# Residual matmuls moved between the gate and up matmuls of a decode kernel, and matmuls into an unread bank in PE's pauses there

## The chip, the cores and the metric

The kernel runs on one core of one Trainium2 chip. The metric is the time of one execution in microseconds of device time, as the median of several runs. A profile of one execution is there as well; all times with a decimal point that are called positions count from the first instruction of that execution.

## The reference

One decode step of a transformer block for 4 sequences (B = 4), one new token each, model width D = 576. The attention has 32 query heads and 16 key/value heads of 128, over the last 4096 of 16384 cached positions. Then follows a gated feed-forward layer of width F = 4608 with a ReLU gate.

```python
def _A_ref(x, k_cache, v_cache, wq, wo):
    W = min(4096, max(256, Sk // 4))
    q = (x @ wq).reshape(B, Sq, Hq, Dh).transpose(0, 2, 1, 3)
    k = jnp.repeat(k_cache[:, :, Sk - W:, :], rep, axis=1)
    v = jnp.repeat(v_cache[:, :, Sk - W:, :], rep, axis=1)
    scores = jnp.einsum("bhqd,bhkd->bhqk", q, k) * (Dh ** -0.5)
    p = _softmax(scores, axis=-1)
    o = jnp.einsum("bhqk,bhkd->bhqd", p, v)
    return o.transpose(0, 2, 1, 3).reshape(B, Sq, Hq * Dh) @ wo

def _B_ref(x, W_gate, W_up, W_down):
    gate = jnp.einsum("bsd,df->bsf", x, W_gate)
    up = jnp.einsum("bsd,df->bsf", x, W_up)
    gate = gate * (gate > 0)
    return jnp.einsum("bsf,fd->bsd", gate * up, W_down)

h = x + _A_ref(_layernorm(x), k_cache, v_cache, wq, wo)
h2 = h + _B_ref(_layernorm(h), W_gate, W_up, W_down)
```

Inputs and the output are bf16.

## The kernel before

The kernel is written engine by engine. Each of the five engines (SP, ACT, DVE, POOL, PE) has a function that issues its instructions in a fixed order, and a small class, Sched, turns the named dependencies into semaphore waits. Nothing is reordered by a planner: the order in prog_pe is the order on PE.

All large transfers are issued by prog_sync on SP's queue, one after the other, into one large SBUF buffer named pool: wq, then K and V of 32 pairs of heads, then wo in four parts, W_gate and W_up in four chunks of 128 rows of D each (named wg and wu, 0 to 3, alternating), then their last 64 rows (wg 4, wu 4), and at last W_down in nine pieces (wd 0 to 8). The first two pieces of W_down hold 9 chunks of 128 rows each, the next five 3 chunks each, and the last two hold 2 and 1. A transfer waits only for the buffer that it overwrites; for W_down that is the end of the output projection, called ATTN.

PE's work has these stages. First it computes q. Then it goes through the 32 pairs of heads: qk multiplies the transposed keys with the queries (matmuls of 512 columns into the four banks of the tile sc), and pv multiplies the probabilities with the values. The operand that holds the queries is the bf16 tile qz. After the last batch of heads comes the output projection, the statistics of the second layer norm, and then the feed-forward layer:

- For c from 0 to 3, 36 matmuls for the gate and 36 for the up projection, each with 128x128 weights and 4 moving columns, all into bank GUB. Each group of 36 waits for its own chunk of weights (`land((kind, c))`).
- Two groups of 18 matmuls with 8 moving columns, for the last 64 rows, gate and then up. The last one is named GU 4. ACT waits for it, applies the ReLU (A_GATE), and DVE multiplies (D_HHT) to make the tile hhT.
- Six fp32 matmuls that put the residual h, transposed back from the tile R_sb by the identity ident_f, into the banks DNB and DNB + 1. R_sb is there since the output projection (D_R).
- The down projection: 36 chunks of F, two matmuls each (one for each half of D, 288 columns, weights hhT of 128x4), which add to the residual in the two banks. The first waits for hhT and for wd 0; each further piece of W_down has its own wait.

At the end ACT and DVE copy one half each to bf16, and SP stores the result. Bank QR is the last of the four banks of sc; it holds the scores until the last softmax has read them, (EXP, 7, 1), and nothing reads it after that.

All matmuls other than the transposes are issued by the helper mm, so they share one line in the profile (L482), and are told apart by their tiles: pb<-hnT,pool and pb<-hn,pool are gate and up, pb<-ident_f,R_sb is the residual, pb<-pool,hhT the down projection.

Of the kernel before, what the change touches and what calls it, by code (L numbers as in the profile page):

```python
# [12 lines left out]
B = 4  # L13
D = 576
# [8 lines left out]
DC = 5  # L23
NDUO = B * KVH // 2
NB = 4
NBATCH = NDUO // NB
# [12 lines left out]
PVLAG = 5  # L39
JJ = 3  # L40
GD = 3
BIG = 1.5e38
NG = FC // JJ
HALF = F // 2
HD = D // 2
# [57 lines left out]
def bass_sequential_preLN__sliding_block_cached__glu_gated_reglu__decode_kernel(  # L103
# [12 lines left out]
    with ExitStack() as es:  # L116
        cnt = [0]

        def sb(name, shape, dt):
            return es.enter_context(nc.sbuf_tensor(name, shape, dt))  # L120
# [4 lines left out]
        ident_f = sb("ident_f", [128, 128], FP32)  # L125
# [17 lines left out]
        qz = sb("qz", [128, 2, NB, 4, 128], BF16)  # L143
# [18 lines left out]
        R_sb = sb("R_sb", [128, 2, DC, B], FP32)  # L162
# [9 lines left out]
        pb = [sc[:, i * 512:(i + 1) * 512] for i in range(4)]  # L172
        pb += [es.enter_context(nc.psum_tensor(f"pb{i}", [128, 512], FP32))[:, :] for i in range(4, 8)]
        PVB, OB, QB, QR, TPB = 4, 6, 6, 3, 7
        OSB, WOB, STB, GUB, DNB = 0, 1, 2, 7, 4
# [50 lines left out]
        for c in range(4):  # L226
            for k, (kind, W) in enumerate((("wg", B_W_gate), ("wu", B_W_up))):
                add((kind, c), f"{kind}{c}", GU0 + (2 * c + k) * ROW, F, None,
                    lambda e, o, c=c, W=W: e.dma_start(out=o, in_=W[c * 128:(c + 1) * 128, :]))
# [4 lines left out]
        wd_sb = pool[:, 0:FC * D].rearrange("p (g x) -> p g x", g=NG)  # L234
        WD = [(0, GD * JJ), (GD * JJ, 2 * GD * JJ)] + [(g * JJ, (g + 1) * JJ) for g in range(2 * GD, NG - 1)] + [(FC - JJ, FC - 1), (FC - 1, FC)]
        for k, (f0, f1) in enumerate(WD):
# [7 lines left out]
        def land(name):  # L244
            return ("L",) + (name if isinstance(name, tuple) else (name,))
# [99 lines left out]
        def prog_dve(S):  # L345
# [17 lines left out]
            for x in range(2):  # L363
# [3 lines left out]
                                              axis=AX.X, op=ALU.add), name="M0")  # L367
            S.op(v, lambda e: e.tensor_scalar(out=mask[:, 1, :], in0=mask[:, 0, :], scalar1=2 * BIG, scalar2=-BIG, op0=ALU.mult, op1=ALU.add),
                 deps=["M0"], name="M1")
            S.op(v, lambda e: e.tensor_scalar(out=mask[:, 2, :], in0=mask[:, 0, :], scalar1=-2 * BIG, scalar2=BIG, op0=ALU.mult, op1=ALU.add),  # L370
                 name="M2")
# [106 lines left out]
        def prog_pe(S):  # L478
            t = "tensor"

            def mm(o, l, r, start, stop, deps=(), name=None, skip=False):
                S.op(t, lambda e: e.matmul(o, lhsT=l, rhs=r, start=start, stop=stop, skip_group_check=skip),  # L482
                     deps=deps, name=name, signal=name is not None)

            for k, (src, base) in enumerate(((xn_bf, 0), (x_bf, 32))):
                for c in range(DC):
                    w = 128 if c < 4 else 64
# [3 lines left out]
                        deps=["A_XN", "IDB", land("x")] if k == 0 and c == 0 else [], name="TP1" if last else None, signal=last)  # L491
            mm(pb[STB][:, 0:B], dup[:, :], x4[:, :], True, True, deps=["D_XNT", "DUP"], name="XDUP")
            first = True
            for c in range(4):
                s = at[("wq", c)]
                for h in range(H):
                    mm(pb[QB][:, h * B:(h + 1) * B], pool[:, s + h * DH:s + (h + 1) * DH], xnT[:, c, :], first, False,
                       deps=[land(("wq", c))] + (["D_XNT"] if first else []) if h == 0 else [], skip=True)
                    first = False
            s = at[("wq", 4)]  # L500
            for h in range(H // 2):
                o = pb[QB][:, 0:H * B].rearrange("p (u x) -> p u x", u=2)[:, :, h * B:(h + 1) * B]
                mm(o, pool[:, s + h * DH:s + (h + 1) * DH], xn4[:, :, :], False, h == H // 2 - 1,
                   deps=[land(("wq", 4)), "XN41"] if h == 0 else [],
                   name="QMM" if h == H // 2 - 1 else None, skip=True)
            for ce in range(4):
                mm(pb[QR][:, ce * 128:(ce + 1) * 128], sel[:, ce, :, :].rearrange("p g k -> p (g k)"), qT_sb[:, :], True, True,
                   deps=["D_QT", "SEL3"] if ce == 0 else [], name="QREP" if ce == 3 else None)
# [55 lines left out]
            for e_ in range(4):  # L564
                for h4 in range(4):
                    mm(pb[OSB][32 * h4:32 * h4 + 32, e_ * 32:(e_ + 1) * 32], ident_b[:, e_:128:4],
                       oT_all[:, :, :].rearrange("p (q h) b -> p h q b", h=4)[:, h4, :, :], True, True,
                       deps=[("NORM", b) for b in range(B)] if e_ == 0 and h4 == 0 else [],
                       name="OSEL" if e_ == 3 and h4 == 3 else None)
            for g in range(NWO):  # L570
                wv = pool[:, at[("wo", g)]:at[("wo", g)] + ROW].rearrange("p (q e n) -> p q e n", q=2, e=4)
                deps = [land(("wo", g))] + (["D_OX"] if g == 0 else [])
                for n in range(DC):
                    w = 128 if n < 4 else 64
                    for q in range(2):
                        for e_ in range(4):
# [3 lines left out]
                            deps = []  # L580
            mm(pb[STB][:, 128:168], ones_f[:, :], R_sb[:, :, :, :], True, True, deps=["D_R"], name="STAT")
            mm(pb[STB][:, 256:256 + B], dup[:, :], hnT[0:64, 4, :], True, True, deps=["N2"], name="HDUP")
            first = True
            gub = pb[GUB][:, 0:2 * FC * B].rearrange("p (u x) -> p u x", u=2)

            def cols(ap, fc):
                g, j = divmod(fc, JJ)
                x0 = g * 128 * JJ + j
                return ap[:, x0:x0 + 127 * JJ + 1:JJ]

            for c in range(4):
                for u, kind in ((0, "wg"), (1, "wu")):
                    s = at[(kind, c)]
                    for f in range(FC):
                        mm(gub[:, u, f * B:(f + 1) * B], cols(pool[:, s:s + F], f), hnT[:, c, :], first, False,
                           deps=[land((kind, c))] + (["N2"] if first else []) if f == 0 else [], skip=True)
                        first = False
            for u, kind in ((0, "wg"), (1, "wu")):
                o = gub[:, u, :].rearrange("p (v x) -> p v x", v=2)
                for f in range(FC // 2):  # L600
                    last = u == 1 and f == FC // 2 - 1
                    mm(o[:, :, f * B:(f + 1) * B], cols(pool[:, at[(kind, 4)]:at[(kind, 4)] + HALF], f), hn4[:, :, :], False, last,
                       deps=[land((kind, 4)), "HN41"] if f == 0 else [], name=("GU", 4) if last else None, skip=True)
            first = True
            for u in range(2):
                for c in range(DC):
                    lo, hi = max(c * 128, u * HD), min(c * 128 + 128, D, (u + 1) * HD)
                    if lo < hi:
                        w = 128 if c < 4 else 64
                        mm(pb[DNB + u][0:B, lo - u * HD:hi - u * HD], R_sb[0:w, 0, c, :], ident_f[0:w, lo - c * 128:hi - c * 128],  # L610
                           c * 128 <= u * HD, False, deps=["D_R", "IDF"] if u == 0 and c == 0 else [], skip=True)
            for k, (f0, f1) in enumerate(WD):
                deps = [land(("wd", k))] + (["D_HHT"] if k == 0 else [])
                for f in range(f0, f1):
                    g, j = divmod(f, JJ)
                    for u in range(2):
                        last = f == FC - 1
                        mm(pb[DNB + u][0:B, 0:HD], hhT[:, f, :], wd_sb[:, g, j * D + u * HD:j * D + (u + 1) * HD], False, last,
                           deps=deps, name=f"DOWN{u}" if last else None, skip=True)
                        deps = []  # L620

        progs = [("gpsimd", prog_pool), ("sync", prog_sync), ("scalar", prog_act), ("vector", prog_dve), ("tensor", prog_pe)]
        S.begin(False)
        for _, p in progs:
# [33 lines left out]
```

## Time and profile before

| | |
|---|---|
| median of 3 runs | 384.68 us (384.5, 384.68, 385.1) |
| the profiled execution's own time | 385.3 us |
| its span, first to last instruction | 383.5 us |
| mean granted TensorE clock | 0.907 |
| busy: PE, DVE, ACT, POOL | 75%, 52%, 13%, 2% of the span |
| read from HBM | 159.58 MB, 416 GB/s over the span |
| down projection | 72 matmuls in 10.5 us, mean record 315 ns |
| gate and up, 4 columns | 288 matmuls, 8.8 us busy, 9.8 us idle before them |

The profiled execution's time has 1.8 us that lie outside its span. [...] The granted clock is the share of full speed at which TensorE ran; a table by stretches of time gives it for any stretch that one asks for. Records of matmuls overlap; the time that one costs in a row is the distance of their starts.

### The profile page before, as it was taken

To read this page: it belongs to the slowest core of one execution; us is meant where nothing else is said; L and a number is where in the kernel's file an instruction comes from. 1 tells how busy PE (TensorE), PEld (TensorE's weight loads), DVE (VectorE), ACT (ScalarE), POOL (GpSimd) and SP (SyncE) were. 2 spreads that over 40 slices of the span, in tenths; PEclk is the share of its full clock that TensorE was granted. 3 is DMA by queue.
4 is the path that set the end of the run, shared out by engine and by line. 5 is a ranking of instruction groups with operands and counts; after the bars stand their busy time and mean duration, and the time that the engine had idled before them with its cause. 6 is when DMAs were issued, how large, how long until landed. Compare 5 with 4: busy or idle time off the path is not lost.

```text
span 383.5 us, 4157 instructions
## 1 busy us (share of the span) xinstructions
PE 288.7 (75%) x1827; PEld 130.2 (34%) x1842; DVE 198.8 (52%) x181; ACT 51.5 (13%) x125; POOL 7.9 (2%) x20
## 2 busy tenths in 40 slices
PE   0059649976996699679958994899499788874387
PEld 0053213322432243224322431343134233374355
DVE  0259789269437854774486558645855450011000
ACT  4021040021102110311030004100400021100000
POOL 4000000000000000000000000000000000000000
PEclk9999958998999899989998999899989998955559
DMA  7999999999999999999999999999999999999994
GB/s 316 426 424 426 431 424 432 426 424 431 426 424 434 424 427 431 426 427 431 426 427 434 424 424 434 427 424 432 427 424 434 426 423 434 403 417 424 414 415 172
DMA packets 14306, 159.86 MB, mean 417 GB/s; under 512 B 1480, under 2 KB 1616, under 8 KB 4560
## 3 DMA queue, kind: packets, MB, share of 16 engines
q1 hardware_dynamic: 14280, 159.59, 98.6%
q8 instruction: 14, 0.23, 0.2%
q10 hardware_dynamic: 8, 0.00, 0.0%
q14 instruction: 4, 0.03, 0.0%
HBM read 159.58 MB, written 0.00 MB: 416 GB/s over the span
## 4 chain that ended last, share of the span: by engine, by line
PE 41%; DMA 23%; issue 15%; DVE 14%; ACT 5%; POOL 1%; SPq 0%; POOLq 0%
PE sc L482 23%; PE pb L482 18%; DMA pool<-in_A_k_cache_dram 9%; DMA pool<-in_B_W_down_dram 7%; DMA pool<-in_A_wo_dram 7%; ACT P L323 4%; DVE kT L394 4%; DVE probT L413 4%; DVE rmx L397 4%; POOL bcm L274 1%; DVE bias L409 0%; DVE rowsum L418 0%; DVE t L405 0%; DVE pmax L400 0%; DVE bmin L407 0%
## 5 line engine op out<-in xcount | busy, mean ns | idle before, releaser
L394 DVE STREAM_TRANSPOSE kT<-pool 128x2048 f32<-128x2048 f32 x64 | 144.5, 2291 | 54.6 <-DMA pool<-in_A_k_cache_dram 49.4
L482 PE MATMUL sc<-kT,qz 128*128 128x512 bf16 x497 | 131.9, 418 | 51.2 <-DVE kT L394 47.6
L482 PE MATMUL pb<-pool,prob 128*16 128x512 bf16 x512 | 116.4, 386 | 0.8 <-DMA pool<-in_A_v_cache_dram 0.8
L482 PEld LDWEIGHTS sc<-kT,qz 128*128 128x128 bf16 x512 | 49.0, 102 | 130.9 <-DVE kT L394 57.0
L482 PEld LDWEIGHTS pb<-pool,prob 128*16 128x16 bf16 x512 | 43.5, 91 | 71.0 <-issue 15.3
L323 ACT ACTIVATE P<-sc,bias 128x512 f32<-128x512 f32 x32 | 22.2, 714 | 176.5 <-DVE bias L409 176.5
L397 DVE TENSOR_REDUCE rmx<-sc 128x2 f32<-128x2048 f32 x8 | 18.3, 2292 | 34.0 <-PE sc L482 34.0
L413 DVE STREAM_TRANSPOSE probT<-P 128x2048 f32<-128x2048 f32 x8 | 18.5, 2311 | 7.8 <-ACT P L323 7.8
L482 PE MATMUL pb<-hnT,pool 128*128 128x4 bf16 x288 | 8.8, 167 | 9.8 <-DMA pool<-in_B_W_up_dram 5.0
L489 PE MATMUL pb<-ident_b,xn_bf 4*128 4x4 bf16 (+1 forms) x5 | 0.4, 175 | 20.3 <-ACT xn_bf L287 20.3
L308 ACT COPY cp<-pb 128x512 f32<-128x512 f32 x8 | 4.7, 584 | 67.5 <-PE pb L482 67.5
L482 PEld LDWEIGHTS pb<-hnT,pool 128*128 128x128 bf16 x288 | 8.2, 104 | 10.3 <-DMA pool<-in_B_W_up_dram 5.2
L422 DVE RECIPROCAL rs_sb<-pb 128x32 f32<-128x32 f32 x4 | 1.4, 338 | 19.8 <-PE pb L482 19.8
L482 PE MATMUL pb<-selT,cp 128*128 128x16 f32 x64 | 7.9, 255 | 4.3 <-ACT cp L308 4.3
L473 DVE TENSOR_TENSOR hhT<-pb,gate_sb 128x144 bf16<-128x144 f32 x1 | 0.3, 308 | 20.9 <-ACT gate_sb L339 20.9
L330 ACT CAST prob<-probT 128x1024 bf16<-128x1024 f32 x8 | 8.4, 1044 | 19.0 <-DVE rs L416 19.0
L482 PE MATMUL pb<-pool,hhT 128*4 128x288 bf16 x72 | 10.5, 315 | 0.4 <-DMA pool<-in_B_W_down_dram 0.4
L482 PEld LDWEIGHTS pb<-selT,cp 128*128 128x128 f32 x64 | 8.2, 191 | 6.3 <-ACT cp L308 5.3
L274 POOL PARTITION_ALL_REDUCE bcm<-pmax x8 | 3.1, 386 | 290.6 <-DVE pmax L400 290.6
L301 ACT COPY qz<-qrep 32x64 bf16<-32x64 bf16 x32 | 7.8, 245 | 7.3 <-DVE qrep L431 7.0
L482 PEld LDWEIGHTS pb<-pool,hhT 128*4 128x4 bf16 x72 | 6.6, 93 | 4.3 <-DMA pool<-in_B_W_down_dram 0.7
L489 PEld LDWEIGHTS pb<-ident_b,xn_bf 4*128 4x128 bf16 (+1 forms) x5 | 0.3, 108 | 20.3 <-ACT xn_bf L287 20.3
(94 smaller groups left out, 71.5 us busy)
## 6 DMA issues: line engine op xcount, KB each, us to landing
pool<-in_A_k_cache_dram SPq DMA_DIRECT2D x32, 2048.0 KB, 28.1
pool<-in_A_v_cache_dram SPq DMA_DIRECT2D x32, 2048.0 KB, 26.1
pool<-in_A_wo_dram SPq DMA_DIRECT2D x4, 1152.0 KB, 21.7
pool<-in_B_W_gate_dram SPq DMA_DIRECT2D x4, 1152.0 KB, 25.7
pool<-in_B_W_up_dram SPq DMA_DIRECT2D x4, 1152.0 KB, 24.5
pool<-in_A_wq_dram SPq DMA_DIRECT2D x4, 1024.0 KB, 7.9
pool<-in_B_W_down_dram SPq DMA_DIRECT2D x2, 1296.0 KB, 27.2
pool<-in_B_W_down_dram SPq DMA_DIRECT2D x5, 432.0 KB, 14.5
```

Of the source, the lines that this page charges most:

```text
L274: S.op(g, lambda e, n=n: e.partition_all_reduce(bcm[:, n % 2, :], pmax[:, n % 2, :], 128, bass_isa.ReduceOp.max), deps=deps, name=("PAR", n))
L301: S.op(a, lambda e, src=src, dst=dst: e.copy(out=dst, in_=src), deps=deps, name=("QZ", n) if g == 3 else None, signal=g == 3)
L308: S.op(a, lambda e: e.copy(out=cp[:, n % 2, :], in_=pb[PVB + n % 2]), deps=deps, name=("CP", n))
L323: S.op(a, lambda e, n=n, th=th, u=u: e.activation(out=P[:, th * 1024 + u:(th + 1) * 1024:2], in_=sc[:, th * 1024 + u:(th + 1) * 1024:2], f ...
L330: S.op(a, lambda e, n=n: e.copy(out=prob[:, n % 2, :, :, :], in_=probT[:, :, 0:NHB].rearrange("p t (r x) -> p r t x", x=4)), deps=deps, na ...
L394: S.op(v, lambda e: e.transpose(out=dst, in_=src), deps=deps, name=("TR", i))
L397: S.op(v, lambda e: e.tensor_reduce(out=rmx[:, n % 2, :], in_=sc[:, :].rearrange("p (x u) -> p u x", u=2), axis=AX.X, op=ALU.max), deps=[( ...
L413: S.op(v, lambda e: e.transpose(out=probT[:, :, :].rearrange("p t j -> p (t j)"), in_=P[:, :]), deps=[("EXP", n, 1)] + ([("CMP", n - 1)] i ...
L422: S.op(v, lambda e: e.reciprocal(out=rs_sb[:, b, :], in_=pb[OB][:, 64 + b * H:64 + (b + 1) * H]), deps=[("SUM", b)], name=("RS", b))
L473: S.op(v, lambda e: e.tensor_tensor(out=hhT[:, :, :], in0=pb[GUB][:, FC * B:2 * FC * B].rearrange("p (f b) -> p f b", b=B), in1=gate_sb[:, ...
L482: S.op(t, lambda e: e.matmul(o, lhsT=l, rhs=r, start=start, stop=stop, skip_group_check=skip), deps=deps, name=name, signal=name is not None)
L489: S.op(t, lambda e, c=c, w=w, src=src, base=base: e.transpose(out=tpv[0:w, base + c * 4:base + (c + 1) * 4], in_=src[0:B, c * 128:c * 128 ...
```

## The change

The residual's six matmuls become a function, residual(u), that is called for u = 0 just ahead of the gate matmuls of chunk 3 and for u = 1 just ahead of its up matmuls. A new function, warm(k), issues k bf16 matmuls of 128x128 weights and 512 columns, both operands taken from qz, into bank QR, which nothing reads any more. Its only dependency is the last softmax's reading of that bank. It is called with the numbers of the list WARM: the first after each of the two halves of the residual, the second ahead of the last gate group, the third ahead of the last up group, and the fourth ahead of the down projection. The list sums to seven; as its first number is used twice, eight such matmuls are issued. No other engine's program changes, and the order of everything else on PE stays.

```diff
+WARM = (1, 1, 2, 3)
...
+            def warm(k):
+                for _ in range(k):
+                    mm(pb[QR], qz[:, 0, 0, 0, :], qz[:, 1, 0, :, :].rearrange("p c m -> p (c m)"), True, True,
+                       deps=[("EXP", NBATCH - 1, 1)], skip=True)
+
+            def residual(u):
+                first = True
+                for c in range(DC):
+                    lo, hi = max(c * 128, u * HD), min(c * 128 + 128, D, (u + 1) * HD)
+                    if lo < hi:
+                        w = 128 if c < 4 else 64
+                        mm(pb[DNB + u][0:B, lo - u * HD:hi - u * HD], R_sb[0:w, 0, c, :], ident_f[0:w, lo - c * 128:hi - c * 128],
+                           c * 128 <= u * HD, False, deps=["D_R", "IDF"] if first else [], skip=True)
+                        first = False
+
             for c in range(4):
                 for u, kind in ((0, "wg"), (1, "wu")):
                     s = at[(kind, c)]
+                    if c == 3:
+                        residual(u)
+                        warm(WARM[0])
                     for f in range(FC):
                         mm(gub[:, u, f * B:(f + 1) * B], cols(pool[:, s:s + F], f), hnT[:, c, :], first, False,
                            deps=[land((kind, c))] + (["N2"] if first else []) if f == 0 else [], skip=True)
                         first = False
             for u, kind in ((0, "wg"), (1, "wu")):
                 o = gub[:, u, :].rearrange("p (v x) -> p v x", v=2)
+                warm(WARM[1 + u])
                 for f in range(FC // 2):
                     last = u == 1 and f == FC // 2 - 1
                     mm(o[:, :, f * B:(f + 1) * B], ...
-            first = True
-            for u in range(2):
-                for c in range(DC):
...
-                        mm(pb[DNB + u][0:B, lo - u * HD:hi - u * HD], R_sb[0:w, 0, c, :], ident_f[0:w, lo - c * 128:hi - c * 128],
-                           c * 128 <= u * HD, False, deps=["D_R", "IDF"] if u == 0 and c == 0 else [], skip=True)
+            warm(WARM[3])
             for k, (f0, f1) in enumerate(WD):
                 deps = [land(("wd", k))] + (["D_HHT"] if k == 0 else [])
```

## The prediction

> **What bounds the kernel now.** I read the page's strip of slices first. DMA is saturated in every slice but the first and the last, and PE's clock, at full speed or near it through the attention, falls to half for the end.
>
> ```profile
> PEclk9999958998999899989998999899989998955559
> DMA  7999999999999999999999999999999999999994
> ```
>
> Then the chain of waits, its last pieces (start, us, what):
>
> ```profile
> 343.77 26.88 DMA pool<-in_B_W_down_dram
> 370.64 0.04 issue
> 370.69 10.55 PE pb L482 x72
> 381.24 0.02 issue
> 381.26 0.45 DVE out_sb L475
> ```
>
> Until 370.64 the transfers set the time. From there the 72 matmuls of the down projection run without a pause. The last piece of W_down is issued at 367.93 and its row gives 12.2 us to landing, so it is there at 380.13; PE ends at 381.24. What can be gained or lost lies in this tail, and depends on PE's clock in it.
>
> Third, the table by stretches. The clock changes at 336.35 and 373.90, which are 37.55 us apart, eleven times 3.413; the changes during the attention fit the same grid. So I cut the trace into cells of 3.413 us (columns: stretch, length, PE busy, PEld, DVE, ACT, POOL, granted clock, DMA share, GB/s).
>
> ```profile
> 49.63:53.05 3.42, 1.93 (x5) 0.73 (x6) 2.71 (x2) 2.11 (x7) 0.00 (x0) 0.50 1.03 441
> 53.05:56.46 3.41, 1.67 (x4) 0.30 (x2) 3.38 (x4) 1.93 (x5) 0.00 (x0) 0.50 1.00 423
> ```
>
> ```profile
> 278.33:281.74 3.41, 2.81 (x7) 1.00 (x8) 1.83 (x2) 0.00 (x0) 0.00 (x0) 0.50 1.02 432
> 281.74:285.15 3.41, 3.41 (x16) 1.27 (x15) 3.22 (x2) 0.00 (x0) 0.00 (x0) 1.00 0.98 418
> ```
>
> ```profile
> 339.77:343.18 3.41, 3.34 (x96) 3.20 (x93) 0.00 (x0) 0.00 (x0) 0.00 (x0) 0.50 1.02 424
> ...
> 363.66:367.07 3.41, 1.77 (x54) 1.60 (x54) 0.00 (x0) 0.00 (x0) 0.00 (x0) 0.50 1.02 412
> 367.07:370.49 3.42, 2.75 (x30) 1.63 (x30) 0.31 (x1) 0.29 (x1) 0.00 (x0) 0.50 1.02 417
> 370.49:373.90 3.41, 3.21 (x14) 1.76 (x15) 0.00 (x0) 0.00 (x0) 0.00 (x0) 0.50 1.02 411
> 373.90:377.31 3.41, 3.41 (x30) 2.34 (x28) 0.00 (x0) 0.00 (x0) 0.00 (x0) 1.00 0.94 377
> ```
>
> What a cell did decides the clock of the next. The cell at 339.77 is busy for 3.34 us with matmuls 4 columns wide and stays at half: time in which columns stream counts, not busy time. A share of 1.93/3.41 = 0.57 did not raise the clock, 2.81/3.41 = 0.82 did. The threshold lies between. The cell at 367.07 narrows it: the residual matmuls stream 1.92 us (below), the 18 narrow ones 0.12, together 0.60, and the clock stays at half. So between 0.60 and 0.82; 0.70 is my middle.
>
> The rates, from the timeline:
>
> ```profile
> 368.10 2.17 PE L482 MATMUL pb<-ident_f,R_sb 128*4 128x128 f32 x12
> ...
> 370.88 1.89 PE L482 MATMUL pb<-pool,hhT 128*4 128x288 bf16 x7
> ...
> 375.18 1.39 PE L482 MATMUL pb<-pool,hhT 128*4 128x288 bf16 x10
> ```
>
> At half clock (1.89 - 0.447 of the last one)/6 = 0.2405 us from start to start, 0.835 ns a column; at full clock (1.39 - 0.286)/9 = 0.1227.
>
> **Check of the tail.** The clock rises 3.21 us after the first down matmul: 13.4 matmuls at half clock, 58.6 x 0.1227 = 7.19, and 0.16 until the last result: 370.69 + 3.21 + 7.19 + 0.16 = 381.25; measured 381.24. Each us more at half clock costs 1 - 0.1227/0.2405 = 0.49 us. The floor: the second piece is issued at 346.27 and lands after 27.5 (the longest of its rows), 373.8; its matmuls and all behind it, 54 x 0.1227 = 6.63, plus 0.16, give 380.6; the last piece at 380.13 and its two matmuls give the same. So up to about 1.9 us at half clock are free, and the most that any clock can save here is 381.24 - 380.6 = 0.65 us.
>
> **The change, part by part.** *Residual moved.* Six fp32 matmuls, recorded as 12 passes with 1152 columns at twice 0.835 ns: 1.92 us (row: 2.17 with the tail of the last). In two halves of 0.96 they now stand ahead of the gate and the up matmuls of chunk 3. Their inputs are ready since 344.2, and only PE's queue is concerned. They used to run from 368.10 to 370.27, while PE waited for 370.64: moving them out saves nothing on the path. *Added matmuls.* The list says 1, 1, 2, 3, and its first entry is issued twice: eight of 512 columns, 512 x 0.835 = 0.43 us each at half clock. Ahead of gate and up of chunk 3 the pauses are 1.66 us, and 0.96 + 0.43 = 1.39 fits. Ahead of chunk 4's gate the pause is 0.32: 0.11 late. Ahead of its up 0.77: two take 0.85, and the up matmuls end about 0.2 late, at 368.4. Relu (0.29) and product (0.31) follow, so hhT is there at 369.1, covered until 370.64; without that cover it would be 0.2 us. The last three end by 369.7, before anything waits for PE. So all the inserted work is free, at 0, and no transfer moves.
>
> *The clock.* In the profile's own cells the new content of 367.07 to 370.49 is: two fillers from 367.07 on 0.6, narrow 0.12, three fillers 1.28: 2.0 us, 0.58, no more than the 0.60 before. It would stay at half, the next cell (filled from 370.69) raises the clock at 373.90 as now, and the change is worth nothing. But this rests on where the grid lies. Call x the time from the first down matmul to the next cell edge (3.21 in the profile). [...] I take x as anything from 0 to 3.41; the timed runs, from 384.5 to 385.1, leave room for this.
>
> Before, the cell that ends at x holds the residual's 1.92 close ahead of the down matmuls: (2.04 + x)/3.41 up to x = 0.8, then above 0.8. At a threshold of 0.70 the clock rises at x for every x above 0.36, and half of these are within the free 1.9 us; the mean loss over the floor is about 0.2. After, the fillers give less, and 1.0 us of idle PE lies ahead of the down matmuls: the share is 0.52 at x = 0, about 0.64 from 0.9 to 2.3, then x/3.41. For x below about 1.7 the clock comes a cell later, 3.4 to 5.1 us after the first matmul, 0.75 to 1.6 over the floor (mean 1.15); between 1.7 and 2.3 the cell before holds 0.70 and may just raise it, at the floor; above 2.4 it is as before (about 0.5). Weighted: 0.52 x 1.15 + 0.30 x 0.5 = 0.75, or 0.55 more than before. A threshold of 0.63 gives 0.3 more, one of 0.77 gives 0.75. I take 0.45. On the median of 384.68 that is 385.1. (The profiled execution took 385.3 for a span of 383.5, 1.8 outside it; its floor would be 384.65, and 384.5 is the fastest timed run, so the median sits just above the floor.)
>
> [...]
>
> **The rivals.** *It works as filler:* the fillers raise the clock in nearly every execution before 372.5, and PE ends at the floor: 384.5, 0.2 under the median. For: with a threshold near 0.60 the plateau of 0.64 is enough. Against: the row with 0.60 that wasn't. Chance 0.24, of which 0.06 that the comparison's runs of before lie as high as the profiled one, so that it shows as over 0.2%. *Clearly slower:* the threshold is 0.75 or more, so that nothing short of the down matmuls raises the clock, and the moved residual takes away what did: for x from 0.7 to 2.7 the clock comes 4.1 to 6.1 us after the first matmul, 1.1 to 2.0 over the floor: about 385.9. It decides from a threshold of 0.74. Chance 0.28. *Nothing happens:* x is always near the profile's; 384.7. Chance 0.08. *My forecast,* a loss under 0.2%: 0.40.
>
> **The numbers.** 0.2%, 0.77 us, is about what a measurement of this kernel can tell from no change; the gain is bounded at 0.65 us, the loss at about 1.9. Faster 0.06; within 0.18 + 0.08 + 0.40 = 0.66; slower 0.28. The range goes from just under the floor, 384.4, to the third case's 386.0; my forecast's own range is 384.8 to 385.4.
>
> **What would show it.** In the profile after: the fillers inside the former pauses; the chain still ending with W_down and 72 matmuls from 370.7; hhT before 369.2; a cell with a share under 0.60 never followed by clock 1.00, one over 0.82 always; the matmuls' end at 381.25 - 0.49 x (3.21 - time at half clock), never under 380.6. Wrong would be: a first down matmul later than 370.8, a transfer that lands elsewhere, a clock that rises after cells that stream under 0.6, or a time under 384.2.

## The result and the profile after

The changed kernel takes 385.64 us (median of 14 runs, 384.59 to 386.39), the kernel before 384.69 (14 runs beside it, 384.31 to 385.36). The medians are 0.95 us apart; the ratio, which is that of the means, is 1.0021 with a 95% interval of 1.0013 to 1.0030: about 0.8 us slower. The forecast was 385.1 in a range of 384.4 to 386.0: the direction and the mechanism are the ones forecast, the size was put at half.

The profiled execution of the changed kernel took 385.91 us, with a span of 384.1. Its chain of waits ends as before (start, us, what):

```profile
343.73 26.70 DMA pool<-in_B_W_down_dram
370.42 0.04 issue
370.46 11.40 PE pb L483 x72
381.86 0.02 issue
381.88 0.45 DVE out_sb L476
```

No transfer and no wait is late: the first piece of W_down is there at 370.42 (370.64 before), and the first down matmul starts with it. But the 72 matmuls take 11.40 us in place of 10.55. The table by cells of 3.413 us, cut at this execution's own clock changes (337.86 and 375.40, 37.54 us or eleven cells apart), says why (columns as in the tables above; the granted clock is the third figure from the end):

```profile
361.75:365.16 3.41, 3.41 (x69) 2.24 (x70) 0.00 (x0) 0.00 (x0) 0.00 (x0) 0.50 1.00 404
365.16:368.58 3.42, 3.16 (x56) 1.80 (x55) 0.28 (x1) 0.29 (x1) 0.00 (x0) 0.50 1.03 418
368.58:371.99 3.41, 2.19 (x9) 0.85 (x8) 0.03 (x1) 0.00 (x0) 0.00 (x0) 0.50 1.02 410
371.99:375.40 3.41, 3.41 (x16) 1.78 (x14) 0.00 (x0) 0.00 (x0) 0.00 (x0) 0.50 1.03 417
375.40:378.82 3.42, 3.42 (x30) 2.37 (x28) 0.00 (x0) 0.00 (x0) 0.00 (x0) 1.00 0.71 282
```

The edge after the first down matmul is at 371.99, so x is 1.53 here. The cell that ends there holds the end of the fillers (to about 369.0), a pause, and 1.5 us of down matmuls; it streams about 2.0 us, a share of 0.58, and the clock is 0.50 for a whole further cell. PE runs 4.94 us at half clock in place of 3.21.

### The profile page after: what moved, and what is told of

It reads as the page before. It is cut to its first block, busy times and chain, and to the rows that moved or that the text cites. A ratio compares the mean times of both kernels' runs of the same rounds, so it can differ in the third digit from the quotient of the medians.

```text
span 384.1 us, 4171 instructions
## 1 busy us (share of the span) xinstructions
PE 297.7 (78%) x1833; PEld 133.1 (35%) x1850; DVE 199.0 (52%) x181; ACT 51.5 (13%) x125; POOL 7.9 (2%) x20
## 4 chain that ended last, share of the span: by engine, by line
PE 46%; DVE 18%; issue 15%; DMA 14%; ACT 6%; POOL 1%; POOLq 0%
PE sc L483 25%; PE pb L483 22%; DMA pool<-in_B_W_down_dram 7%; DMA pool<-in_A_wo_dram 7%; DVE kT L395 6%; ACT P L324 5%; DVE probT L414 4%; DVE rmx L398 4%; POOL bcm L275 1%; DVE bias L410 0%; DVE rowsum L419 0%; DVE pmax L401 0%; DVE t L406 0%; DVE bmin L408 0%; ACT qz L302 0%
## 5 line engine op out<-in xcount | busy, mean ns | idle before, releaser
L483 PE MATMUL sc<-kT,qz 128*128 128x512 bf16 x497 | 134.8, 426 | 47.9 <-DVE kT L395 44.4
L483 PE MATMUL pb<-pool,prob 128*16 128x512 bf16 x512 | 118.0, 391 | 0.0
L483 PE MATMUL pb<-pool,hhT 128*4 128x288 bf16 x72 | 11.4, 331 | 1.2 <-DMA pool<-in_B_W_down_dram 1.2
L483 PE MATMUL pb<-selT,cp 128*128 128x16 f32 x64 | 8.7, 269 | 4.3 <-ACT cp L309 4.3
L483 PEld LDWEIGHTS pb<-selT,cp 128*128 128x128 f32 x64 | 9.0, 208 | 6.3 <-ACT cp L309 5.3
```

## The experiments

Two theories. The share theory is the prediction's: the clock is granted cell by cell, by the share of the cell before in which columns stream, and what the change does is to empty the cell ahead of the down projection by moving the residual out of it. (A filler is one of the matmuls that `warm` issues; x is, as in the prediction, the time from the first down matmul to the next cell edge.) The rival, called the filler theory, is that the fillers cost time themselves, by holding PE's queue or by disturbing the transfers.

**e1: the residual moved, no fillers.**

```diff
-WARM = (1, 1, 2, 3)
+WARM = (0, 0, 0, 0)
```

> The change's residual in its new places, all eight fillers left out. Share theory (a 3.413 us cell decides the next cell's clock by the share in which columns stream, threshold between 0.62 and 0.82, and the residual's move emptied the cells ahead of the down projection): only the down matmuls themselves can raise the clock, so it is as slow as the change or a little slower, 0.9 to 1.1 us over the floor of 384.4 on average against 0.2 to 0.4 before: 385.5, and single runs spread over about 1.7 us. Filler theory (the eight fillers cost time themselves, by holding PE's queue or disturbing the transfers): without them it is as before, 384.7.

Measured: 385.45 (384.57 to 386.35), ratio to before 1.0016, interval 1.0002 to 1.0030. Most or all of the loss is there without any filler, which is against the filler theory. The interval only just leaves 1 out; e4 below decides. In its profile:

```profile
369.21:372.63 3.42, 2.24 (x10) 1.24 (x11) 0.00 (x0) 0.00 (x0) 0.00 (x0) 0.50 1.03 412
372.63:376.04 3.41, 3.41 (x16) 1.81 (x15) 0.00 (x0) 0.00 (x0) 0.00 (x0) 0.50 1.02 412
376.04:379.45 3.41, 3.41 (x30) 2.36 (x28) 0.00 (x0) 0.00 (x0) 0.00 (x0) 1.00 0.55 214
```

The down matmuls start at 370.39 and fill 2.24/3.41 = 0.66 of the cell, and the next cell is still at 0.50. Behind that one, which is full, the clock is 1.00.

**e2, e3, e4, e7, e8: the stretch ahead of the down projection made dense again.** e2 puts the residual back behind the last up matmuls and keeps the five fillers ahead of it:

```diff
-                        residual(u)
                         warm(WARM[0])
...
+            residual(0)
+            residual(1)
             warm(WARM[3])
-WARM = (1, 1, 2, 3)
+WARM = (1, 1, 2, 0)
```

> The residual back in its old place behind the last up matmuls; five fillers (1, 1, 1, 2) in the pauses ahead of it, none behind it. Share theory: the residual's 1.92 us stream just ahead of the down matmuls again, and the fillers before it add to the same cells: mean 0.1 to 0.25 over the floor, 384.6 (as before or 0.1 faster). Filler theory: five of the eight fillers keep five eighths of the loss, 385.2.

e3 is e2 with one filler behind the residual:

```diff
-WARM = (1, 1, 2, 0)
+WARM = (1, 1, 2, 1)
```

> As e2 with one filler more behind the residual, so that PE streams without a pause from the last up matmuls to the first down matmul. Share theory: every place of the grid has a cell with a share over 0.82 that ends before or soon after the first down matmul: every run at the floor, 384.4, with a spread of 0.3 us or less, 0.3 us faster than before. Filler theory: slower than before, 385.3.

e4 leaves the change as it is and fills the last pause whole:

```diff
-WARM = (1, 1, 2, 3)
+WARM = (1, 1, 2, 6)
```

> The change with six fillers ahead of the down projection in place of three, so that the idle 1.2 us there are filled too. Share theory: a run of 2.6 us of fillers and then the down matmuls: every cell that ends after 370.5 has a share over 0.8: all runs at the floor, 384.4, 1.2 us faster than the change. Filler theory: eleven fillers in place of eight, slower than the change: 385.9 or more.

e8 is the kernel before with one filler behind the residual (e3 with `WARM = (0, 0, 0, 1)`):

> The kernel before with one filler behind the residual and nothing else. Share theory: the 0.4 us pause ahead of the first down matmul is closed; mean 0.1 over the floor, 384.55, single runs up to 385.0, and 0.1 faster than before, at the limit of what the runs can tell. Filler theory: a filler that holds PE at half clock until 370.75 delays the first down matmul: 0.1 slower than before.

And e7 is e4 without the fillers in the earlier pauses:

```diff
-WARM = (1, 1, 2, 6)
+WARM = (0, 0, 0, 6)
```

> The change with the residual in its new places, no fillers in the pauses of the gate and up matmuls, and six fillers ahead of the down projection. Share theory: the five early fillers do nothing that matters and the last pause alone decides; mean 0.06 over the floor, 384.5, no run over 384.9, 1.1 us faster than the change. Filler theory: six of eight fillers keep three quarters of the loss: 385.3. A theory in which the clock has to be raised during the gate and up groups: as slow as the residual moved without fillers, 385.5.

Measured (12 runs each; e1 to e4 beside 35 runs of the kernel before with a median of 384.72, e7 and e8 beside 23 others with 384.98):

| | median us | ratio to before | 95% interval |
|---|---|---|---|
| the change | 385.64 | 1.0021 | 1.0013 to 1.0030 |
| e1, residual moved, no fillers | 385.45 | 1.0016 | 1.0002 to 1.0030 |
| e2, residual back, five fillers | 384.53 | 0.9992 | 0.9980 to 1.0004 |
| e3, and one behind it | 384.51 | 0.9992 | 0.9979 to 1.0005 |
| e4, the change, last pause full | 384.50 | 0.9988 | 0.9977 to 0.9999 |
| e7, only the last pause, full | 384.70 | 0.9990 | 0.9977 to 1.0003 |
| e8, before, one behind | 384.50 | 0.9986 | 0.9973 to 0.9999 |

Three more fillers in the last pause take the change from 0.8 us slower to at least as fast as before: more added work, less time, the contrary of the filler theory. e2, e3 and e8 lie 0.2 to 0.5 us under the kernel before beside them, where the share theory had 0.1 to 0.3; only e8's interval leaves 1 out. All 12 runs of e4 lie between 384.40 and 384.74, where the change's spread over 1.8 us; of e3's runs 11 lie between 384.44 and 384.65 and one, which I can't explain, at 386.36. e7 is 0.9 us faster than the change without the early fillers, so the last pause decides most of it. But three of its runs lie above the 384.9 that I had set as its bound, up to 385.63. Its profile shows a part of the reason: x is 2.43, the cell ahead of the one with the down matmuls (365.96 to 369.37) holds only 1.66 us of fillers, a share of 0.49, and the clock comes 2.43 us after the first down matmul. By the same counting, and with a bound of 0.70, I estimate that every x from 1.9 to about 3.1 costs e7 up to 0.6 us, which I had overlooked, and that in e4, with the two fillers of the pause before, this ends at about 2.2. What lies above 385.0 remains open; the kernel before also scattered more beside e7 (up to 385.93 but for one). In e4's profile, the cells and then the chain's end:

```profile
367.64:371.06 3.42, 3.42 (x15) 1.14 (x12) 0.31 (x1) 0.29 (x1) 0.00 (x0) 0.50 1.03 412
371.06:374.47 3.41, 2.99 (x25) 1.87 (x24) 0.00 (x0) 0.00 (x0) 0.00 (x0) 1.00 1.02 417
```

```profile
373.37 0.04 issue
373.42 6.92 PE pb L483 x54
380.34 0.02 issue
```

The cell that ends at 371.06 is full of fillers and down matmuls, and the clock is 1.00 from its end on, 0.8 us after the first down matmul. PE then catches up with the transfers: its last 54 matmuls wait for the second piece of W_down, at 373.37. That is the prediction's floor, which stands at 380.34 here and not at 380.6: the second piece landed 0.4 us before the 373.8 that the prediction took. So the prediction's sign that PE would never end under 380.6 was wrong by 0.26. e4 and e8 may beat the kernel before as well, by 0.1%, but their intervals only just leave 1 out, and the runs beside them include one of the kernel before at 387.16 (e4) and at 387.33 (e8) that weighs in these ratios.

**e5 and e6: the threshold by itself.** Behind the last down matmul of the kernel before stand stretches (sixteen in e5), each one repeated pattern of long matmuls with m matmuls of 4 columns between them, and 4-column matmuls alone between the stretches. The core of e5, with matmuls that write the unread bank:

```diff
+            def stretch(kind, m):
+                for _ in range(int(10.5 / (0.427 + 0.0288 * m)) + 1):
...
+                    small(m)
+                small(550)
```

> The kernel before, with a measurement behind its last down matmul (its time is some 300 us longer and says nothing): fifteen stretches of about 10.5 us, each a repeated unit of one long matmul and m matmuls of 4 columns, with 10 us of 4-column matmuls between stretches. Eight stretches have 512 bf16 columns on 128x128 weights with m = 12, 10, 8, 7, 6, 5, 4, 3 (shares of streaming of about 0.56, 0.60, 0.65, 0.68, 0.72, 0.76, 0.80, 0.84), four have 512 columns on 128x4 weights and four an fp32 matmul of 128 columns on 128x4 weights (m = 8, 6, 5, 4). Share theory: no rise of the clock in the stretches below a share that lies between 0.62 and 0.82, about 0.77 by the spread of the timed runs, a rise in all above it, and the same for the three kinds. Against it: a rise at all shares or at none (then something other than the share counts), or other thresholds for 4-column weights or fp32 (then the width of the weights or the type counts too).

> A second measurement behind the kernel before (its time says nothing). The first sweep puts the threshold at 0.69 to 0.70 for 512 columns on 128x128 weights, if the 4-column matmuls between them are left out of the share. Here: three stretches of that kind again (m = 9, 8, 7), five with three 512-column matmuls on 128x4 weights in a row and m = 20, 14, 10, 6, 2 small ones behind them (shares of about 0.63, 0.69, 0.73, 0.78, 0.85), five with three fp32 matmuls of 128 columns on 128x4 weights and the same m, and four stretches of nothing but matmuls of 16, 24, 32 and 48 columns. Share theory: one threshold of about 0.69 for all kinds. If 4-column weights or fp32 count for less, their rise comes only at a higher share or at m = 2. The last four tell what a short matmul counts for: if every streamed column counts, 24 columns (0.69 of 28.8 ns) is at the edge and 32 and 48 raise the clock; if short ones count nothing, 16 to 32 don't.

Shares here are taken from the distances of the long matmuls' starts: 0.427 us (512 columns at half clock) over that distance, the small ones not counted. In e5 with 128x128 weights, a cell of m = 8 (0.640 us, 0.67; 453.44 to 456.85) was followed by a clock of 0.50, one of m = 6 (0.587, 0.73; 501.22 to 504.64) by 1.00. Of m = 7 (0.613, 0.70), the first whole cell was followed by 0.50 and the second by 1.00:

```profile
477.33:480.74 3.41, 3.40 (x48) 1.98 (x48) 0.00 (x0) 0.00 (x0) 0.00 (x0) 0.50 0.02 5
480.74:484.16 3.42, 3.20 (x44) 1.81 (x44) 0.00 (x0) 0.00 (x0) 0.00 (x0) 0.50 0.00 0
484.16:487.57 3.41, 3.33 (x109) 2.93 (x109) 0.00 (x0) 0.00 (x0) 0.00 (x0) 1.00 0.02 5
```

Counted by the starts within each cell instead of by the pattern, these two hold 0.67 (no) and 0.70 (yes). In the steady patterns of e5 the bound therefore showed near 0.70, between 0.67 and 0.73, not at the 0.77 that I had read from the spread of the timed runs with the narrow matmuls counted in.

In the kernel itself the line was less sharp. In the profile of the change, a cell of the attention that streams 512-column matmuls for 2.62 of 3.41 us, 0.77, was followed by a clock of 0.50:

```profile
54.55:57.96 3.41, 2.62 (x7) 0.94 (x8) 3.41 (x3) 0.20 (x1) 0.00 (x0) 0.50 0.99 418
57.96:61.38 3.42, 3.42 (x10) 1.17 (x9) 3.42 (x2) 0.00 (x0) 0.00 (x0) 0.50 1.07 455
```

And up to the last down matmul e5 and e6 are two more executions of the kernel before. In e5 (first three rows) the first down matmul starts at 370.92, so x is 0.60, and the cell with the residual holds (1.92 + 0.60)/3.41 = 0.74 by the prediction's count without the narrow ones; the clock comes a whole cell later, after 4.01 us. In e6 (last two rows) the first starts at 370.37, x is 1.06, the cell holds 0.81, and the clock comes at its end:

```profile
368.10:371.52 3.42, 2.95 (x25) 1.57 (x22) 0.31 (x1) 0.29 (x1) 0.00 (x0) 0.50 1.03 420
371.52:374.93 3.41, 3.41 (x16) 1.78 (x14) 0.00 (x0) 0.00 (x0) 0.00 (x0) 0.50 1.03 410
374.93:378.34 3.41, 3.41 (x29) 2.38 (x28) 0.00 (x0) 0.00 (x0) 0.00 (x0) 1.00 0.86 344
```

```profile
368.01:371.43 3.42, 3.02 (x17) 1.54 (x16) 0.31 (x1) 0.19 (x1) 0.00 (x0) 0.50 1.02 416
371.43:374.84 3.41, 3.12 (x26) 1.96 (x24) 0.00 (x0) 0.00 (x0) 0.00 (x0) 1.00 1.03 411
```

So the kernel before, too, paid for a late clock in one of its executions: 4.01 us at half clock in e5's, beside 1.06 in e6's. Counted by recorded starts, cells between 0.70 and 0.77 went either way: 0.70 and 0.73 (e5) were followed by 1.00, 0.74 (e5) and 0.77 (the change) by 0.50.

The 4-column weights and the fp32 matmuls of e5 told nothing, as PE's change from long to small ones cost 0.18 us more there and no share came over 0.60. With three in a row in e6, a cell with 0.67 (128x4 weights, 497.72 to 501.13) was followed by 0.50, cells with about 0.71 (fp32, 593.29 to 596.71) and 0.74 (128x4, 473.83 to 477.24) by 1.00, as with the 128-column weights of e5 (0.67 by 0.50, 0.73 by 1.00). The last two are of the patterns with m = 20, whose mean share is only 0.64 but of which one cell caught two groups of three almost whole: here the clock went by the cell, not by the mean. Of the short ones, 24 columns back to back left the clock at 0.50, and behind 32 it was 1.00:

```profile
740.07:743.48 3.41, 3.41 (x133) 3.41 (x129) 0.00 (x0) 0.00 (x0) 0.00 (x0) 0.50 0.02 5
763.96:767.37 3.41, 3.41 (x133) 3.41 (x130) 0.00 (x0) 0.00 (x0) 0.00 (x0) 0.50 0.02 5
767.37:770.79 3.42, 2.96 (x119) 2.88 (x116) 0.00 (x0) 0.00 (x0) 0.00 (x0) 1.00 0.02 5
```

The first row is one of 24 columns, the second one of 32: both busy to the full, with 133 records each, whose starts are about 26.7 ns apart (in place of the 28.8 expected). At 0.835 ns a column, 24 columns would stream 20 of the 26.7 ns, 0.75, and did not raise the clock, although the steady pattern of long matmuls with 0.73 did. So in these runs columns alone did not tell short matmuls from long ones.

## Why the prediction was right in direction and short in size

**The tail formula held.** First down matmul, time at half clock c, and the end by 0.2405 and 0.1227 us a matmul plus 0.16, beside the measured end:

| | start | c | formula | measured |
|---|---|---|---|---|
| the change | 370.46 | 4.94 | 381.87 | 381.86 |
| e1 | 370.39 | 5.65 | 382.15 | 382.13 |
| e3 | 370.52 | 1.98 | 380.48 | 380.54 |
| e7 | 370.36 | 2.43 | 380.55 | 380.53 |
| e8 | 370.58 | 1.76 | 380.44 | 380.66 |

In e8 the down matmuls stop twice, after the 18th for 0.10 us and after the 60th for 0.14, each time where the next piece of W_down is needed; that is its 0.2 over the formula. Where the clock came sooner (e2 at 0, e4 at 0.8 us), PE ended at 380.43 and 380.34, the floor.

**The inserted work was free, as said.** The last up matmuls of the profiled execution end at 367.9, hhT is there at 368.6, the fillers are through at 369.2, and the first down matmul waits only for its data. The pause ahead of it, 1.22 us in the trace, is the one that the prediction put at 1.0.

**The grid lay elsewhere in every profile.** Counted in steps of 3.413 us from the changes of the clock, the edge after the first down matmul came 3.21 us behind it in the profile before, and 1.53, 2.24, 1.98, 0.80, 2.43 and 1.76 in those of the change, e1, e3, e4, e7 and e8; in e5 and e6 it was 0.60 and 1.06. That x takes every value from 0 to 3.41 alike, as the forecast's weights have it, was my assumption, and no run shows it; the profiles show these nine values, from 0.60 to 3.21. The spread of the change's 14 runs, 384.59 to 386.39, fits an x that differs from run to run: by the tail formula each us at half clock costs 0.49.

**What failed is the weighting that led to 0.45.** The middle threshold, 0.70, is where e5's steady patterns parted (0.67 without a rise, 0.73 with one), and the sum at it was already 0.55. But its shares held the narrow gate and up matmuls, 0.12 us for each group, and these counted for little: the cell at 339.77 before, 3.34 us busy with 4-column matmuls (records of 166 ns, starts 27 ns apart), was followed by 0.50, and with the 24 columns of e6 the clock stayed at 0.50. With them the cell before the last seemed to reach 0.70 for x between 1.7 and 2.3 and to bring some executions to the floor. Without them it holds at most the five fillers of the last two pauses, 5 x 0.427 = 2.13 us, a share of 0.62, and I take it as never raising the clock. No profile of the change has its grid there, so this step is argued and not shown.

The same sum at 0.70 is then: after, for x below 2.4 (70% of places) the clock comes a cell later and costs 0.49 x (1.2 + 3.41 - 1.88) = 1.34 us on average; above it 0.5; together 0.94 + 0.15 = 1.09. Before, the residual's cell needs x above 0.47 now; 0.12 for the 14% below it, which the prediction's 0.2 left out, and 0.17 for the late places give 0.29. The difference is 0.80 us; measured, 0.21% or 0.81. That it agrees so closely is luck: in e5's execution x = 0.60 was not enough, and with a bound at 0.8 in place of 0.47, and at 2.7 in place of 2.4, the same sum gives 0.39, 1.24 and a difference of 0.85. The rounding down from 0.55 to 0.45 and the mean over thresholds that were equally open made the rest of the shortfall.

**The rivals.** "It works as filler" did not come: in the profile no cell short of the down matmuls reached 0.70 with the fillers as placed. "Clearly slower" named the outcome rightly, that nothing short of the down matmuls raised the clock and the moved residual took away what did, but gave as its reason a threshold of 0.75 or more. Cells of e5 and e6 with 0.70 to 0.74 were followed by 1.00, which speaks against that; the change's own cell of 0.77, followed by 0.50, speaks for it, so its reason is not fully settled. Its 385.9 is 0.3 over the measured median. "Nothing happens" needed an x that is always near 3.21; the profiles show 0.60 to 3.21.

## What to carry to other kernels

Where PE idles on transfers ahead of its last long stretch, look at the clock in the trace, cell by cell, and not at busy time alone. In the profiles of the kernel before and of the change, with matmuls of 32 columns and more counted at 0.835 ns a column (fp32 at twice that), the 19 cells at half clock that were followed by full clock stream 0.81 of their length or more, and no other cell at half clock streams over 0.78; in e5 and e6 single cells of 0.70 to 0.74 went either way. In this kernel, PE filled from 366.2 on without a hole (e4) put all twelve runs at or under 384.74; with only the 2.6 us ahead of the down projection filled (e7), the clock came 2.43 us after its first matmul in the profile, and single runs took up to 385.63. The residual looked movable at no cost, as it was off the chain of waits, and moving it alone took the time from 384.72 to 385.45 all the same (e1); with the hole filled (e4) it was 384.50. So a move that looks free is worth a run by itself, and a look at what the moved work leaves behind it. Three fillers in a pause that needed six made no difference that the runs show (1.0021 with the fillers, 1.0016 with none).

## What was not expected of the hardware

In e6, matmuls of 24 columns back to back, with PE busy to the full (3.41 of 3.41 us), left the clock at 0.50, and behind those of 32, with starts at the same 26.7 ns, it was 1.00. 4-column weights and fp32 passes went with the clock as 128-column bf16 weights of about the same streaming time did, as far as e6's cells at 0.67, 0.71 and 0.74 and e5's at 0.67 and 0.73 tell.

The clock fell at another share than it rose. In the profiles of the kernel before and of the change, counting matmuls of 32 columns and more at 0.417 ns a column (fp32 at twice that), the 19 cells at full clock that were followed by half clock stream 0.33 of their length or less, and of the other cells at full clock none streams under 0.35. That is how the clock of the tail was lost: in the kernel before, the cell that ends at 336.35 has a clock of 1.00 and streams 0.33, its longest pause of PE is 0.72 us, the next cell has a clock of 0.50, and no later cell short of the down matmuls reaches 0.70.
